# A fixed order table, two more pairs of chunks by seven block products, and six chunks converted early in an attention and two-MLP kernel

## The chip, the core and the metric

The kernel runs on one core of one Trainium2 chip. The metric is the device time of one execution in microseconds, lower is better. Before the change it is 782.16 us, the median of three runs (780.87 to 784.16).

## The reference

Memory attention with 32 slots is followed by a leaky MLP and a bilinear MLP, all in float32. `k_m` and `v_m` are per head 32 rows of 64; the second half is three large products over 2304 tokens.

```python
a = softmax(phi, axis=seq)                       # 4 x 8 x 576 x 32
k_m, v_m = a^T @ k, a^T @ v                      # per head 32 x 64
x = softmax(q @ k_m^T / 8) @ v_m                 # -> 2304 x 512
h = x @ w_in;  x = max(0.01 * h, h) @ w_out      # 512 -> 2048 -> 512
out = ((x @ w_a) * (x @ w_b)) @ w_out2           # 512 -> 1536 -> 512
```

## The kernel before

A product of two float32 matrices is done as three passes: each operand is split into a rounded high part and the rest, and high x high, high x low and low x high are summed in PSUM (`PASSES`). A split costs one copy (ACT or DVE) and one subtraction (DVE). Weights come from DRAM as 64-bit numbers and are turned into float32 by two ACT and four DVE instructions for each 128x512 piece (`weight`: high, low, clamp, shift, join, add), then split.

There are three stages. The first is attention (0 to about 60 us), batch by batch. `kv_part` loads phi, k and v, takes the maximum over the sequence (`nmx`, DVE), the exponential (ACT), transposes (`ta`, `tz`, PE), multiplies (`km`), scales (`kvn`), transposes again (`kvt`) and copies the result into `kd` and `vm`; `sc_both` makes the scores, whose softmax (`sm`, with the helpers `mx` and `sr`) ends in the tile `at`. The tokens of a batch come in two pieces, of 320 and 256 columns. The second stage is the first MLP (to about 375 us): `vw` folds `v_m` into `w_in`, `h_unit` makes a block of h, `y_unit` multiplies it by `w_out`. The third is the second MLP over 12 chunks of 128 of its 1536 columns and over two halves `s` of the tokens; the columns of 64 tokens of each batch that are left over go through `left_unit`. `ab_unit` makes both inner products of a chunk with seven block products, `abx`, `aby` and `abz`, instead of eight.

The last product, with `w_out2`, takes two chunks at a time. Where `by_seven(s, c)` is false, `o_unit` does it directly: 8 outputs of 6 passes of 512 columns. Where it is true, `p_sums` and `w2_sums` build sums of blocks of both factors, and `o_part` multiplies them with seven products for each of two row halves (3 passes each) and spreads them over the accumulators:

```python
SEVENS = ((8, 9, 10, 11), tuple(range(10)))      # chunks by seven, for s = 0 and s = 1
O_PARTS = ((1, "A11", "B11"), (2, "A12", "B21"), (6, "S2", "T2"), (7, "S3", "T3"), (4, "A22", "T4"), (5, "S1", "T1"), (3, "S4", "B22"))
```

`p_sums` forms T1 to T4 with four subtractions and splits seven operands; `w2_sums` loads the float32 weights again (`wf`), makes four sums and splits them.

The first `PRE` chunks of the second MLP have their weights converted during the first MLP, written to DRAM (`keep_weights`) and read back (`w_back`); the others are converted in the third stage.

The order of all of it is not the order of the code. Each operation is recorded with the tiles that it reads and writes (`Program.op`); `Program.order` plays the program through with assumed costs (`c_dve`, `c_act`, `c_pass`, `SLACK`, `NUDGE`), picks at each moment the most urgent operation that is ready and has room, also its engine where two can do it and the room of its tiles, and `run` issues the operations in that order. All transfers are issued by SP in program order, each one waits until the transfer eight places before it has landed. `WARM` transposes of an identity matrix stand at the head of PE's work, and `idle` puts four more behind some early results. An engine works its list strictly in that order.

Of the kernel before, what the change touches and what calls it, by code (L numbers as in the profile page):

```python
# [52 lines left out]
PRE = 5  # L53
# [4 lines left out]
NUDGE = {1: -48.49, 2: -17.57, 3: -0.76, 4: -3.51, 6: -10.66, 9: -0.3, 10: 0.34, 11: 0.67, 12: -0.23, 15: -4.91, 16: 0.37, 19: -0.01, 22: -12.61, 23: -25.92, 24: 6.05, 25: -20.43, 26: 6.22, 29: 5.25, 30: -1.03, 33: -1.08, 34: 0.18, 35: -1.25, 36: 7.2, 38: -0.74, 40: -2.21, 42: -1.91, 44: -0.72, 45: 1.51, 46: 20.7, 47: 4.08, 48: -8.63, 49: 4.68, 50: -23.08, 51: -1.24, 52: 0.28, 54: -12.45, 55: -3.05, 57: -0.08, 58: 4.38, 60: 25.62, 61: -0.19, 62: 1.46, 63: -0.19, 64: 14.35, 65: 17.46, 66: 7.11, 67: -30.82, 68: -2.57, 69: -3.68, 70: 4.08, 71: 2.16, 72: -5.51, 73: 3.76, 74: 11.57, 76: -0.33, 77: 0.8, 81: 2.6, 83: -0.23, 86: 0.21, 88: 16.61, 90: -1.17, 92: -0.59, 96: 4.63, 99: 0.07, 103: 0.97, 106: 14.54, 107: -27.63, 109: 1.17, 110: -2.34, 111: -0.09, 112: -2.83, 113: -0.93, 114: -1.13, 118: -3.12, 119: -12.84, 121: -0.12, 122: -0.26, 124: 1.93, 128: -13.55, 133: -2.46, 135: -0.09, 138: 0.06, 139: -3.54, 145: 1.03, 147: 0.04, 150: -0.64, 154: 2.61, 156: -36.26, 158: 16.1, 159: 1.35, 161: 3.36, 162: -0.42, 164: 4.55, 165: 0.05, 166: -3.77, 168: 0.39, 170: 11.14, 171: -3.97, 172: -5.44, 173: -2.43, 174: 1.13, 176: 0.94, 177: 5.17, 179: -1.18, 180: 0.4, 191: -1.73, 193: 2.21, 194: -0.27, 202: 0.73, 206: 0.97, 210: 0.09, 211: -0.24, 213: 15.62, 218: 2.9, 222: 0.72, 223: -0.03, 224: 1.55, 225: 0.27, 226: 8.51, 227: -0.23, 228: 1.22, 229: -0.49, 230: 9.69, 231: -43.15, 234: 0.36, 236: -1.75, 237: 2.72, 238: -58.33, 239: -1.64, 244: 4.13, 245: 10.87, 246: -44.04, 247: 2.64, 248: -4.48, 250: -0.39, 252: -1.44, 253: -1.5, 254: 0.23, 258: -1.35, 260: 3.26, 265: 9.59, 270: 5.29, 273: -4.26, 275: -9.82, 276: 1.34, 278: -7.31, 280: -6.24, 284: -1.88, 285: 0.18, 290: 1.13, 291: 1.14, 292: -5.63, 294: 1.39, 298: -0.06, 301: -5.57, 302: 0.42, 305: -1.09, 309: -17.67, 310: -0.78, 318: 0.61, 322: -1.59, 323: -0.28, 326: 12.04, 330: -13.23, 331: 1.15, 332: 8.66, 334: 3.29, 335: 7.89, 336: -0.53, 337: -6.49, 338: -2.42, 340: -16.79, 342: 3.52, 343: -0.05, 344: -8.26, 346: -18.18, 347: -0.13, 348: 0.63, 349: -0.21, 351: -2.03, 352: -0.87, 353: -3.55, 354: -0.99, 355: 5.28, 358: -0.8, 360: -2.83, 361: -4.43, 362: -0.31, 364: -0.25, 365: 0.37, 366: -0.51, 368: -0.28, 370: 8.22, 372: 2.75, 376: 6.22, 377: 0.07, 378: -9.41, 382: 9.32, 383: -14.31, 384: 0.6, 388: -0.21, 390: -2.09, 394: 9.89, 396: 0.61, 397: -7.48, 398: 0.4, 400: -16.99, 402: -0.43, 404: -0.91, 406: 6.5, 407: 1.68, 408: -4.78, 410: -0.5, 412: 0.42, 413: 9.97, 414: -2.31, 418: 10.12, 420: -0.66, 421: -0.48, 424: -1.62, 425: 19.33, 426: 3.26, 427: -14.35, 428: -25.92, 430: 8.73, 431: -0.14, 432: 5.62, 434: -0.05, 435: 5.56, 436: 3.43, 438: -0.46, 439: 3.09, 440: 0.69, 441: -1.61, 442: 5.28, 444: -3.22, 445: -1.01, 448: 2.67, 449: -0.8, 450: 4.58, 451: -4.01, 452: 2.12, 454: -4.52, 456: -0.86, 458: -0.99, 462: -1.59, 466: -2.13, 469: -5.99, 470: 0.23, 471: -4.55, 472: -1.36, 474: -6.92, 477: -0.94, 478: -5.9, 488: -1.13, 489: 0.2, 491: -4.41, 492: -0.47, 493: -0.58, 497: 0.08, 500: -7.25, 503: 1.25, 504: -0.9, 506: -0.19, 507: -0.2, 508: 2.0, 510: 1.27, 534: -19.4, 538: -0.38, 542: 14.1, 543: 0.63, 550: 0.74, 551: -0.99, 558: -0.88, 559: -9.51, 561: -0.16, 567: 0.56, 572: -0.2, 1281: 0.97, 1301: 0.22}  # L58
# [8 lines left out]
POOL_BIAS = 19.06
LAT, LAT_SAME, LAT_DMA = 0.427, 0.372, 6.72
OVER = {'DMA': 0.0, 'PE': 0.0, 'ACT': 0.1, 'DVE': 0.058, 'POOL': 0.0}
BLOCKED = 7.16  # L70
# [39 lines left out]
class Program:  # L112
# [13 lines left out]
    def op(self, eng, cost, fn, r=(), w=(), tiles=(), pos=None, ahead=60.0, keep=0, slack=0.0, soon=False):  # L126
        o = Op()
        port = isinstance(eng, Port)
        o.costs = {e: (c - OVER[e]) * SPARE[e] for e, c in (eng if isinstance(eng, dict) else {eng: cost}).items()}
# [23 lines left out]
    @staticmethod  # L153
    def lat(a, b):
        return LAT_DMA if a.eng == "DMA" else LAT_SAME if a.eng == b.eng else LAT

    def urgency(self, target):

        for o in reversed(self.ops):
            t = target.get(o.seq, 1e9)  # L160
            for a in o.after:
                t = min(t, a.late - self.lat(o, a) - o.cost)
            o.late = t - o.slack
        first = {}
        for o in self.ops:
            for k in o.tiles:
                if first.setdefault(k, o) is not o and self.specs[k][0] not in ("slot", "big", "five"):
                    o.late = min(o.late, max(x.late + x.cost for x in o.before) + 2.0)
            if o.soon:
                o.late = min(o.late, max(x.late + x.cost for x in o.before) + 1.0)  # L170

    def order(self, target):
        uses, free, rooms_of = {}, {}, {}
        for o in self.ops:
# [1312 lines left out]
```

## Time and profile before

| | |
|---|---|
| median of three runs | 782.16 us |
| profiled execution, device time | 781.57 us |
| its span, first to last instruction | 779.8 us |
| PE busy | 768.4 us |
| DVE busy | 632.2 us |
| ACT busy | 402.3 us |
| mean granted TensorE clock, of full speed | 0.993 |

The span is what the trace covers; the device time is 1.8 us longer than it. Instructions of one engine are pipelined, so that a busy PE is not by itself a PE at its peak; whether it is has to be read from how far apart its groups of matmuls end. A wait of an engine counts only where PE waits for it in turn.

### The profile page before, as it was taken

How to read it: one execution, taken by the hardware profiler on the slowest of the kernel's cores; microseconds unless marked ns; L12 is line 12 of the kernel's file. 1: busy time of each engine (PE TensorE's matmuls, PEld its weight loads, DVE VectorE, ACT ScalarE, POOL GpSimd, SP SyncE). 2: the span in 40 equal slices, each digit the busy share in tenths (PEclk: the TensorE clock that was granted, in tenths of full speed). 3: DMA queues.
4: the chain of work that ended last, by engine and by line, in shares of the span. 5: the costliest groups of instructions: out<-in, count | busy, mean ns of one | idle time of the engine just before them, and what ended most of it. 6: DMA issues, size and time to landing. Idle time of an engine off the chain costs nothing.

```text
span 779.8 us, 12713 instructions
## 1 busy us (share of the span) xinstructions
PE 768.4 (99%) x4762; PEld 658.2 (84%) x4762; DVE 632.2 (81%) x1205; ACT 402.3 (52%) x856; POOL 0.7 (0%) x6
## 2 busy tenths in 40 slices
PE   7899999999999999999999999999999999999998
PEld 6577898889888988898888888888888888888886
DVE  4897899789788988585742999999899777898876
ACT  4685777667457555453444546454453344444430
POOL 0000000000000000000000000000000000000000
PEclk8999999999999999999999999999999999999999
DMA  9993241755065532035975566584789886556603
GB/s 319 379 311 114 82 163 68 244 174 191 27 231 177 177 106 109 18 108 199 379 276 193 193 215 243 191 296 162 252 266 359 275 289 232 191 193 239 216 1 108
DMA packets 58860, 155.22 MB, mean 199 GB/s; under 512 B 7408, under 2 KB 22768, under 8 KB 58800
## 3 DMA queue, kind: packets, MB, share of 16 engines
q1 hardware_dynamic: 58800, 154.42, 56.2%
q8 instruction: 37, 0.61, 0.3%
q14 instruction: 23, 0.19, 0.1%
HBM read 107.74 MB, written 46.66 MB: 198 GB/s over the span
## 4 chain that ended last, share of the span: by engine, by line
PE 95%; DMA 3%; DVE 1%; SPq 0%; issue 0%
PE y L886 24%; PE abx L1107 17%; PE h L834 12%; PE o L1204 9%; PE abz L1107 8%; PE os_x L1323 5%; PE aby L1107 4%; PE os_z L1323 2%; PE b L1161 2%; PE a L1161 2%; PE y L882 2%; PE vw L765 2%; DMA phi<-in_phiT_dram 1%; PE os_y L1323 1%; DMA raw_win<-in_w_in_dram 1%; PE km L608 1%
## 5 line engine op out<-in xcount | busy, mean ns | idle before, releaser
L886 PE MATMUL y<-g,wout 128*128 128x320 f32 (+2 forms) x1104 | 199.3, 334 | 0.0
L886 PEld LDWEIGHTS y<-g,wout 128*128 128x128 f32 x1104 | 175.3, 188 | 21.1 <-issue 4.7
L1107 PE MATMUL abx<-yb_T,wo 128*128 128x512 f32 x432 | 110.2, 390 | 0.0
L1107 PEld LDWEIGHTS abx<-yb_T,wo 128*128 128x128 f32 x432 | 80.0, 188 | 15.8
L787 ACT ACTIVATE g<-h 128x320 fp32r<-128x320 f32 (+1 forms) x120 | 49.9, 416 | 68.1 <-PE h L834 63.8
L1118 ACT COPY t<-abx 128x512 f32<-128x512 f32 x72 | 42.2, 587 | 74.1 <-PE abx L1107 73.4
L834 PE MATMUL h<-ahi,vwh 128*128 128x320 f32 (+1 forms) x240 | 72.1, 300 | 0.0
L834 PE MATMUL h<-ahi,vwl 128*128 128x320 f32 (+1 forms) x240 | 71.0, 296 | 0.0
L834 PE MATMUL h<-alo,vwh 128*128 128x320 f32 (+1 forms) x240 | 71.0, 296 | 0.0
L905 DVE TENSOR_TENSOR acc<-y,acc 128x320 f32<-128x320 f32 (+1 forms) x72 | 40.1, 557 | 31.4 <-PE y L886 30.3
L850 DVE TENSOR_TENSOR g<-t,g 128x320 fp32r<-128x320 f32 (+1 forms) x120 | 53.8, 454 | 10.3 <-ACT t L787 9.4
L1204 PE MATMUL o<-p,wout 128*128 128x512 f32 (+2 forms) x246 | 59.8, 385 | 0.5 <-DVE osum L1217 0.5
L1204 PEld LDWEIGHTS o<-p,wout 128*128 128x128 f32 x246 | 45.6, 188 | 10.3 <-DVE osum L1217 1.1
L787 ACT ACTIVATE t<-h 128x320 f32<-128x320 f32 (+1 forms) x120 | 49.9, 416 | 1.5 <-PE h L834 1.2
L834 PEld LDWEIGHTS h<-ahi,vwh 128*128 128x128 f32 x240 | 45.4, 189 | 5.1 <-issue 3.0
L834 PEld LDWEIGHTS h<-alo,vwh 128*128 128x128 f32 x240 | 45.4, 189 | 0.2
L834 PEld LDWEIGHTS h<-ahi,vwl 128*128 128x128 f32 x240 | 45.5, 190 | 0.0
L1115 DVE TENSOR_TENSOR t<-abz,t 128x512 f32<-128x512 f32 x48 | 33.0, 687 | 10.5 <-PE abz L1107 5.7
L1343 ACT COPY ok<-os_x 128x512 f32<-128x512 f32 x42 | 24.6, 587 | 25.6 <-PE os_x L1323 23.3
L1107 PE MATMUL abx<-yb_B,wo 128*128 128x512 f32 x144 | 36.9, 391 | 0.0
L1107 PE MATMUL aby<-yb_B,wo 128*128 128x512 f32 x144 | 36.6, 390 | 0.0
L1107 PE MATMUL abz<-yb_B,wo 128*128 128x512 f32 x144 | 36.6, 390 | 0.0
(334 smaller groups left out, 1385.6 us busy)
## 6 DMA issues: line engine op xcount, KB each, us to landing
k_wo<-wo SPq DMA_DIRECT2D x28, 512.0 KB, 3.9
wo<-k_wo SPq DMA_DIRECT2D x28, 512.0 KB, 4.3
raw_wout<-in_w_out_dram SPq DMA_DIRECT2D x23, 512.0 KB, 5.1
raw_win<-in_w_in_dram SPq DMA_DIRECT2D x16, 512.0 KB, 6.4
kv<-in_kv_dram SPq DMA_DIRECT2D x16, 512.0 KB, 10.5
k_yb_T<-yb_T SPq DMA_DIRECT2D x8, 512.0 KB, 6.4
yb_T<-k_yb_T SPq DMA_DIRECT2D x8, 512.0 KB, 7.0
k_wout<-wout SPq DMA_DIRECT2D x7, 512.0 KB, 5.3
```

The source lines that it names most:

```text
L787: nc.scalar.activation(dst, src, AF.Prelu, alpha=0.01)
L834: nc.tensor.matmul(T[o], T[w[u]][:, k, fs], T[a[v]][:, k, cols], start=(k == 0 and i == 0), stop=(k == 1 and i == 2))
L850: lambda T, e: engines[e].tensor_tensor(T[g][:, i, 1, to], T[t], T[g][:, i, 0, to].bitcast(F32), op=ALU.subtract),
L886: nc.tensor.matmul(T[o], w[:, u, here], T[g][:, j, v, at:at + m], start=(f == 0 and p == 0), stop=(f == 3 and p == 2))
L905: "DVE", c_dve(m), lambda T: nc.vector.tensor_tensor(T[acc][:, i, :], T[o], T[acc][:, i, :], op=ALU.add),
L1107: nc.tensor.matmul(T[o], T[w][:, which, u, k * P:(k + 1) * P], T[ys[v]][:, k, :], start=first and k == 0 and x == 0, stop=k == 1 and x == ...
L1115: op("DVE", 0.69, lambda T: nc.vector.tensor_tensor(T[to], T[o], T[x], op=ALU.add), r=[o, x], w=[to], tiles=[o, x, to])
L1118: op("ACT", 0.59, lambda T: nc.scalar.copy(T[t], T[X]), r=[X], w=[t], tiles=[X, t])
L1161: nc.tensor.matmul(T[o], T[w][:, k // 2, u, k % 2 * P:(k % 2 + 1) * P], T[ys[v]][:, k, :], start=(k == 0 and x == 0), stop=(k == 3 and x = ...
L1204: nc.tensor.matmul(T[o], T[w][:, u, es], T[g][:, at, v, here], start=(x == 0 and k == 0), stop=(x == 1 and k == 2))
L1323: nc.tensor.matmul(T[o], lhs(T, u), T[g][:, v, :], start=i in (1, 2, 5) and k == 0, stop=k == 2, skip_group_check=True)
L1343: op("ACT", 0.59, lambda T: nc.scalar.copy(T[k][:, x, :], T[o]), r=[o], w=[(k, x)], tiles=[o, k])
```

## The change

The planner, its costs and `NUDGE` go. Two tables take their place: `ORDER` lists all operations by their number, with a letter for the engine where there is a choice (a ACT, v DVE, g POOL), and `PLACES` the room of each tile. `run` walks the table. Three constants change what is computed where: `SEVENS` gains chunks 0 to 3 for the first half of the tokens, two pairs; `PRE` goes from 5 to 6; `WARM` from 22 to 38 transposes.

```diff
-PRE = 5
+PRE = 6
-WARM = 22
-SEVENS = ((8, 9, 10, 11), tuple(range(10)))
+WARM = 38
+SEVENS = ((0,1,2,3,8,9,10,11), tuple(range(10)))
...
+ORDER = """
+1 238 0 26 24 246 224 25 4 5 23 6 231 239 9 2 3 27 12v 28 241v 46 247 30 31 32v 45 225 240 8 227v 34a 228 64 226 242 249v 248 44 35 243 10a 36 22 250 229 37
...
+PLACES = """
+b4 s6 s26 kvn0 g1 g0 f2 b6 b7 b5 b7 s15 s12 s19 s1 kvn0 s14 f5 b6 b7 b7 b6 s17 s4 f6 s14 kvn0 s19 s24 g5 b5 b7 b7 b5 f5 s25 kvn0 s9 f0 b6 b7 b5 b6 f3 b6 b5
...
+    def run(self, make):
+        rooms = dict(zip(self.specs, PLACES.split()))
+        engine = {"a": "ACT", "v": "DVE", "g": "POOL"}
+        tiles, done = {}, set()
+        for word in ORDER.split():
+            o = self.ops[int(word.rstrip("avg"))]
+            assert o.before <= done and o not in done
+            done.add(o)
             for k in o.tiles:
                 if k not in tiles:
-                    tiles[k] = make(k, got[k], *self.specs[k])
+                    tiles[k] = make(k, rooms[k], *self.specs[k])
             if len(o.costs) > 1:
-                o.fn(tiles, e)
+                o.fn(tiles, engine[word[-1]])
             else:
                 o.fn(tiles)
```

By count of instructions, PE loses 96 matmuls of `o` (128x512) and gains 84 of `os` and 16 transposes `warm`; DVE has 45 instructions more, ACT 9 more, SP 7 transfers more (two of `wf`, five of chunk 5's weights back from DRAM). Nearly every row of every engine stands in another place. Three places follow.

The first is SP, the loads of the opening (names end in a number of the tile; `q_0_0_0` and `q_0_1_0` are the 320 columns of batch 0, `phi_1` and `kv_1` belong to batch 1). Before, from the eighth load on:

```order
L469 DMA raw_win_0_0_131<-in_w_in_dram 128x2x256
L572 DMA kv_0_0_1_146<-in_kv_dram 128x1024
L572 DMA kv_0_0_0_155<-in_kv_dram 128x1024
L469 DMA raw_win_0_1_170<-in_w_in_dram 128x2x256
L666 DMA q_0_1_1_179<-in_qT_dram 128x2x256
L666 DMA q_0_0_1_190<-in_qT_dram 128x2x256
L666 DMA q_0_1_0_200<-in_qT_dram 128x2x320
L666 DMA q_0_0_0_212<-in_qT_dram 128x2x320
L562 DMA phi_1_225<-in_phiT_dram 128x1152
```

After, from the same place on:

```order
L530 DMA kvr_0_146<-in_kv_rest_dram 64x2x512
L621 DMA q_0_0_1_149<-in_qT_dram 128x2x256
L424 DMA raw_win_0_1_152<-in_w_in_dram 128x2x256
L527 DMA kv_0_0_0_158<-in_kv_dram 128x1024
L527 DMA kv_0_0_1_160<-in_kv_dram 128x1024
L517 DMA phi_1_167<-in_phiT_dram 128x1152
L621 DMA q_0_1_1_180<-in_qT_dram 128x2x256
L527 DMA kv_1_1_0_193<-in_kv_dram 128x1024
L621 DMA q_0_1_0_199<-in_qT_dram 128x2x320
L621 DMA q_0_0_0_216<-in_qT_dram 128x2x320
```

`phi_1` moves from the 16th to the 13th load, `q_0_0_0` from the 15th to the 17th, and `kv_0_0` from the 9th and 10th to the 11th and 12th.

The second place is DVE, behind the tile `at_0_1` with which the first MLP starts. Before:

```order
L726 STREAM_TRANSPOSE at_0_1_430<-sm_0_1_313 128x512
L717 TENSOR_REDUCE sr_0_10_84<-sm_0_0_345 128x20
L718 TENSOR_SCALAR sr_0_10_84<-sr_0_10_84 128x20
L719 RECIPROCAL sr_0_10_84<-sr_0_10_84 128x20
L626 TENSOR_SCALAR kvn_1_1_448<-km_1_1_406,er_1_82 128x256
L722 TENSOR_TENSOR sm_0_0_345<-sm_0_0_345,sr_0_10_84 128x640
L482 TENSOR_SCALAR cv_wout_0_0_434<-cv_wout_0_0_434 128x512
L726 STREAM_TRANSPOSE at_0_0_467<-sm_0_0_345 128x640
```

After, from `sm_0_0` on:

```order
L677 TENSOR_TENSOR sm_0_0_363<-sm_0_0_363,sr_0_10_84 128x640
L681 STREAM_TRANSPOSE at_0_0_465<-sm_0_0_363 128x640
L437 TENSOR_SCALAR cv_wout_0_0_460<-cv_wout_0_0_460 128x512
L491 TENSOR_REDUCE nmx_0_77<-phi_2_340 128x2
L437 TENSOR_SCALAR cv_wout_0_1_483<-cv_wout_0_1_483 128x512
L441 TENSOR_SCALAR cv_wout_0_0_460<-cv_wout_0_0_460 128x512
L441 TENSOR_SCALAR cv_wout_0_1_483<-cv_wout_0_1_483 128x512
L491 TENSOR_REDUCE nmx_1_80<-phi_3_344 128x2
L445 SCALAR_TENSOR_TENSOR cv_wout_0_1_483<-raw_wout_0_1_324,cv_wout_0_1_483 128x512
L445 SCALAR_TENSOR_TENSOR cv_wout_0_0_460<-raw_wout_0_0_293,cv_wout_0_0_460 128x512
L368 COPY kd1_75<-kvt_1_0_508 64x64 x2
```

The `kvn` of batch 1 leave DVE (ACT makes them now), both maxima `nmx` come early, and the copies of `kd1`, which were ACT's, stand behind them.

The third place is PE in the third stage, at the first pair of chunks (`abx_0_2` is chunk 2 of the first half, `o_0_0_0_0` the first direct output of chunks 0 and 1). Before:

```order
L1107 MATMUL abx_0_2_4787<-yb_0_B11_0_0_3841,wo_0_2_0_4484 128x512 x2
L1107 MATMUL abx_0_2_4787<-yb_0_B11_1_0_3849,wo_0_2_0_4484 128x512
L1107 MATMUL abx_0_2_4787<-yb_0_B11_0_0_3841,wo_0_2_0_4484 128x512
L1204 MATMUL o_0_0_0_0_4798<-p_0_0_0_4672,wout2_0_0_4505 128x512 x3
L1204 MATMUL o_0_0_0_0_4798<-p_0_1_0_4779,wout2_1_0_4520 128x512 x3
```

After, behind the unit T3 of the same chunk 2:

```order
L1062 MATMUL abx_0_2_4802<-yb_0_T3_0_0_4363,wo_0_2_3_4699 128x512 x2
L1062 MATMUL abx_0_2_4802<-yb_0_T3_1_0_4383,wo_0_2_3_4699 128x512
L1062 MATMUL abx_0_2_4802<-yb_0_T3_0_0_4363,wo_0_2_3_4699 128x512
L1278 MATMUL os_0_0_0_z_4949<-pb_0_0_T1_4814,w2_0_0_0_4779 128x512 x3
L1278 MATMUL os_0_0_0_x_4852<-pb_0_0_T3_4909,w2_0_0_1_4781 128x512 x3
```

In place of units of six matmuls of `o` stand units of three of `os`, spread between those of later chunks.

## Rows read from the trace of the kernel before

**Rows 1.** The page's head, engines and last chain.
```profile
span 779.8 us, 12713 instructions
PE 768.4 (99%) x4762; PEld 658.2 (84%) x4762; DVE 632.2 (81%) x1205; ACT 402.3 (52%) x856; POOL 0.7 (0%) x6
PE 95%; DMA 3%; DVE 1%; SPq 0%; issue 0%
```

**Rows 2.** Windows: length, PE, PEld, DVE, ACT, POOL busy, clock, DMA, GB/s.
```profile
300.00:350.00 50.00, 50.00 (x352) 44.92 (x351) 37.59 (x70) 25.33 (x59) 0.00 (x0) 1.00 0.21 76
350.00:450.00 100.00, 100.00 (x530) 87.11 (x529) 61.00 (x107) 44.32 (x86) 0.00 (x0) 1.00 0.68 249
450.00:600.00 150.00, 150.00 (x797) 129.66 (x796) 139.89 (x269) 71.39 (x131) 0.00 (x0) 1.00 0.70 244
```

**Rows 3.** One window for lines L1107, L1323, L1204 alone: PE and PEld.
```profile
600.00:700.00 100.00, 69.50 (x282) 52.36 (x281) 1.00 0.70 240
600.00:700.00 100.00, 38.84 (x147) 27.39 (x147) 1.00 0.70 240
600.00:700.00 100.00, 3.49 (x24) 3.40 (x24) 1.00 0.70 240
```

**Rows 4.** The last chain in order of time: start, length, what.
```profile
33.01 2.59 PE h L816 x12
37.76 0.70 PE sc L682 x16
38.46 2.35 PE h L816 x8
52.29 2.35 PE y L882 x8
375.88 1.36 PE abz L1107 x6
379.96 1.43 PE a L1161 x12
```

**Rows 5.** Timeline of SP's issues in the opening: start, length, what.
```profile
13.57 0.35 SPq L562 DMA_DIRECT2D phi<-in_phiT_dram  x1
21.11 1.26 SPq L469 DMA_DIRECT2D raw_wout<-in_w_out_dram  x2
24.28 2.08 SPq L660 DMA_DIRECT2D q<-in_qT_dram  x2
33.39 0.33 SPq L660 DMA_DIRECT2D q<-in_qT_dram  x1
```

**Rows 6.** Timeline of DVE in the opening.
```profile
24.28 1.35 DVE L536 TENSOR_REDUCE nmx<-phi 128x2 f32<-128x1152 f32 x1 [1.08 <-DMA phi<-in_phiT_dram]
27.15 0.51 DVE L703 STREAM_TRANSPOSE sm<-sc 128x320 f32<-128x320 f32 x1
31.35 0.48 DVE L626 TENSOR_SCALAR kvn<-km,er 128x256 f32<-128x256 f32 x1 [0.36 <-PE km L608]
31.75 0.70 DVE L726 STREAM_TRANSPOSE at<-sm 128x512 f32<-128x512 f32 x1
34.62 0.42 DVE L482 TENSOR_SCALAR cv_wout<-cv_wout 128x512 f32<-128x512 f32 x1
34.96 0.84 DVE L726 STREAM_TRANSPOSE at<-sm 128x640 f32<-128x640 f32 x1
```

**Rows 7.** Window of the first loads, columns as in Rows 2.
```profile
10.00:20.00 10.00, 8.26 (x93) 5.79 (x93) 6.08 (x15) 5.19 (x13) 0.00 (x0) 0.66 1.05 389
```

**Rows 8.** Timeline of PE at the start.
```profile
1.35 4.95 PE L430 MATMUL warm<-ident 128*128 128x128 f32 x22 [1.35 <-POOL ident masks.py:199]
12.24 1.08 PE L608 MATMUL km<-kv,en 128*32 128x128 f32 x16 [0.41 <-DMA kv<-in_kv_dram]
```

**Rows 9.** DVE groups by form: count, busy, mean ns, idle before.
```profile
L1115 DVE TENSOR_TENSOR t<-abz,t 128x512 f32<-128x512 f32 x48 | 33.0, 687 | 10.5 <-PE abz L1107 5.7 <-ACT t L1118 4.5
L1250 DVE TENSOR_TENSOR w2s<-wf 128x256 f32<-128x256 f32 x14 | 5.6, 419 | 2.6 <-PE abx L1107 2.6
```

More of the change, by code (lines that the diff above doesn't have):

```diff
@@ L1 @@
-from bisect import insort
 from contextlib import ExitStack
-from heapq import heappop, heappush
 import concourse.bass as bass
@@ L66 @@
 BIAS = 0.52
[L67 to L70, printed above, removed]
 DMA_RATE = 355000.0
-SPARE = {'DMA': 1.03, 'PE': 1.0, 'ACT': 1.03, 'DVE': 1.03, 'POOL': 0.92}
 def c_dve(n):
@@ L99 @@
+f5 b4 b3 b4 g1 s28 s25 s24 s26 s14 s28 g5 s6 s20 b7 b2 b5 t2 t4 t0 s4 b4 b3 s14 b4 g2 f6 s6 s8 f3 s6 f5 s10 g5 s22 s15 s13 s19 s15 b6 b2 b5 t1 t3 t2 s19 b4
+b3 b4 s24 s26 s14 g2 s8 s5 s2 f7 s22 g1 b1 b0 b7 t0 t4 t1 f6 s22 b4 b3 s2 b4 g0 g6 s25 s13 s28 s1 s4 b6 b0 b1 t2 t3 t1 s1 f4 b4 b3 b4 b4 b3 b4 b3 b4 b3 b4
+b3 b4 b3
+"""
 class Port(dict):
-    pass
-class NoRoom(RuntimeError):
     pass
@@ L128, in op @@
         port = isinstance(eng, Port)
-        o.costs = {e: (c - OVER[e]) * SPARE[e] for e, c in (eng if isinstance(eng, dict) else {eng: cost}).items()}
+        o.costs = eng if isinstance(eng, dict) else {eng: cost}
         eng = next(iter(o.costs))
@@ L151, in op @@
         return o
[L153 to L170, printed above, removed]
@@ L300, in run @@
-    def run(self, make, rounds=6):
-        main = [o for o in self.ops if o.pos is not None]
-        main.sort(key=lambda o: o.pos)
-        target, t = {}, START
-        for o in main:
-            target[o.seq] = t
-            t += o.cost
-        best, self.tries = None, []
-        for _ in range(rounds):
-            self.urgency(target)
-            try:
-                done, got = self.order(target)
-            except NoRoom:
-                if best is None:
-                    raise
-                break
-            end = max(o.end for o in done)
-            self.tries.append(round(end, 1))
-            if best is None or end < best[0]:
-                best = (end, done, got, [o.eng for o in done])
-                self.best_ops = [(o.start, o.end, o.seq, o.eng, o.tiles) for o in done]
-                self.best_got = got
-            target = {o.seq: o.start for o in main}
-            t = 1e9
-            for o in reversed(main):
-                t = target[o.seq] = min(target[o.seq], t - 1e-3)
-        self.length, done, got, engines = best
-        tiles = {}
-        for o, e in zip(done, engines):
+    def run(self, make):
[6 more added lines that the diff above has]
+            done.add(o)
```

257 lines of the change are left out of this document (129 added, 128 removed).

## The prediction

> **What bounds the kernel now.** I read the page's head first [rows 1]: PE is busy for 768.4 of 779.8 us and carries 95% of the chain that ended last; DVE, with 632.2 us, is next. The reader is to see that only PE's own time, and what PE waits for, can move the end. The clock is no question outside the opening: it is 1.00 in the later windows [rows 2].
>
> A busy PE need not be a PE at its peak, so the next view is the chain in order of time [rows 4]. In the third stage six matmuls of 512 columns take 1.36 us, 0.227 us each, and twelve of 256 columns 1.43, 0.119 each. Counted over 100 us [rows 3], 282 + 147 of the first and 24 of the second kind make 429 x 0.227 + 24 x 0.119 = 100.2 us: no time is left over. PE is at its peak there though DVE is busy for 139.9 of 150 us in one stretch [rows 2]. So from about 33 us to the end each matmul less is worth its whole time, and nothing else can be gained but the opening.
>
> The opening is bound otherwise. SP issues each load when the one eight places before it has landed, so its issues tell landings [rows 5]: the 8th landed at 13.57, `phi_1`, the 16th, at 24.28, the 23rd at 33.39. By the shapes, 3392 KB lie up to the 8th and 9984 KB up to the 23rd, so the loads come at 6592 / 19.82 = 333 KB/us, back to back. DVE waits 1.08 us for `phi_1` [rows 6], and the first unit of the first MLP starts at 33.01 [rows 4], behind the tile `at_0_1`, which DVE ends at 32.45 [rows 6].
>
> **Seven products for two more pairs.** PE loses 96 matmuls of `o` and gains 84 of `os`, all of 512 columns: 12 x 0.227 = 2.72 us less, on the path.
>
> DVE pays for it with some 30 wide instructions more of 0.687 us (subtractions, splits, evictions), 8 sums of 0.419 [rows 9] and a few copies, about 26 us. They fall into the first 100 us of the third stage, where DVE is idle for 39 of 100 us [rows 2]; ACT, idle for 56, takes casts. So I cost them at nothing. If that cover were gone, each `os` unit that comes late by one DVE instruction would cost PE 0.69 us, and four such units would eat the gain.
>
> [...]
>
> **Six chunks early.** Chunk 5's weights need about 11.8 us of DVE (three times clamp, shift, join and add: 6.6; four sums: 1.7; five subtractions: 3.4). They leave the stretch 450 to 600, where DVE is 93% busy, and go before 375, where the last 50 us of the first MLP alone leave 12.4 idle [rows 2]. Five loads of 512 KB more, and two of `wf`, are 3.6 MB, 9.2 us at the 389 GB/s of [rows 7], against a third of 250 us free on the queues [rows 2]. Nothing.
>
> **Sixteen more transposes at the start.** 22 took 4.95 us [rows 8], so 38 end near 9.9 instead of 6.3. Behind them stand transposes of `phi_0`; the products that need those wait for `kv` until 12.24 [rows 8]. Nothing.
>
> **The opening in its new order.** `phi_1` has 896 KB less ahead of it and lands 2.7 us earlier, at 21.6; `q_0_0_0` (landed at about 21.9, since the second issue of the pair at 21.11 waits for it [rows 5]) has 1088 KB more ahead and lands at 25.2. Its scores take 0.70 [rows 4], the two transposes behind them together about 0.93 (0.51 each, overlapping by a tenth [rows 6]), so DVE has `sm_0_0` at about 26.9, against 27.66 before (27.15 + 0.51 [rows 6]). From there to the start of `at_0_1` is 4.1 us before; the `kvn` between them, with its wait 0.76 (31.75 less the 30.99 at which that wait begins [rows 6]), is ACT's now. That ends `at_0_1` near 31.0, 1.4 us earlier. PE also needs the last `kv` of batch 1, the 21st load in both orders: 1024 KB before the 23rd, 30.3, and about one more microsecond for `km`. I put the first unit at 31.4. The like of it before is 33.01 less the `kvt` that is behind it now, 32.6: 1.2 us gained.
>
> Then some is given back. `at_0_0` ends at 35.80 before [rows 6], and with two foreign instructions less between them at about 33.6 after. The copies of `kd1` stand behind two maxima of 1.35 each [rows 6], which wait for `phi_2` and `phi_3`, the 24th and 25th load: 576 KB each behind 33.39, so 35.1 and 36.8. The first maximum ends at 36.5, three instructions of 0.42 [rows 6] at 37.7, the second maximum at 39.1, two joins of 0.69 at 40.4, the copies at 40.9. PE reaches the scores that need `kd1` after four units of 256 columns (0.86 each, from 2.59 for three), three of 320 (1.08), and 1.3 for small transposes: 31.4 + 8.0 = 39.4, and 0.4 for the exponentials of `phi_2`. It waits about 1.1 there, 1.5 in all. Queued behind those scores are `h` and `y` units of batch 0. Before had its own: eight records of 320 columns would take 2.16 by the 256-column rate and take 2.35 [rows 4], in four such pieces, 0.8 us. The opening is worth -1.2 + 1.5 - 0.8 = -0.5 us. Its ends: -2.0 if none of the new waits is there, +3 if the first unit starts 1 us later than before and the waits double.
>
> **The sum.** -2.72 - 0.5 = -3.2 us. The profiled execution took 781.57 us, 0.59 below the median of the runs; 778.35 on its scale is 778.9 on that of the median, -0.4%.
>
> **Rivals.** First, a better opening: none of the waits behind `at_0_0`, since the loads run ahead of 333 KB/us when small pieces of `q` no longer stand together. Then -2.72 - 2.0: 777.4. For it speaks that `phi_1` frees DVE early; against it that `q_0_0_0` and `phi_3` are landings, which an order on DVE doesn't move.
>
> Second, the matmuls go but their time stays: `os` units come in runs of three, and each change between two accumulators or a late `pb` makes PE wait 0.2 us or so, 56 units at 0.05 being enough. Then only the opening counts: 781.7. [...] Against it, `os` units stand in the window of [rows 3] at the full rate.
>
> Third, slower: DVE in the first 28 us. The maximum of `phi_0_1`, the fourth load now (1600 KB, so near 8.2), stands second on DVE, and all conversions of `w_in` behind it, about 11 us of work from 9.0 on. Back to back they end near 20, before `phi_1`. But DVE was busy for only 6.08 of 10 us in that stretch [rows 7]; at that share they end at 27.2, and `kvn`, `kd0`, the scores and `at_0_1` come 7 us later: 782.16 - 2.72 + 7.1 = 786.5. It decides from 6.6 us in the opening. Against it: by 9 us most of what DVE waited for has landed.
>
> **How the numbers follow.** A change of 0.5%, 3.9 us, is about what a measurement of this kernel can tell from none: faster is below 778.25, slower above 786.07. The forecast, 778.3 to 780.8 of its own, has 0.45; the better opening 0.32; the time that stays 0.15; the slow DVE 0.08. Faster is the second case and a little of the first: 0.33; slower 0.08; the rest 0.59. The range reaches from 776.2, a microsecond below the better opening, to 783.0, above the third case; the slow DVE is left out.
>
> **What would show it.** 84 more `os` and 96 fewer `o` matmuls with the spacing of 1.36 us per six unchanged. The first `h` unit near 31.4 and the copies of `kd1` near 41, with the scores waiting on them. DVE in the first 100 us of the third stage near 87% and PE still without a gap. It is wrong if PE shows waits on `pb` tiles or ACT there, if the first `h` unit starts after 33, or if the count above leaves more than 1 us of a 100 us window over.

## The result and the profile after

The kernel after takes 786.28 us (784.79 to 790.43) against 781.79 (the median of seven executions; the 782.16 at the head is that of three): ratio 1.0063, interval 1.0040 to 1.0086. A second measurement (e8 below) gave 784.55 us, ratio 1.0044 [1.0027, 1.0061]. It is slower by 3.4 to 4.9 us, where 3.2 less was forecast. The profiled execution took 787.23 us.

The page's head of the kernel after, which answers to [rows 1]:

```profile
span 785.5 us, 12755 instructions
PE 769.0 (98%) x4766; PEld 656.6 (84%) x4766; DVE 650.9 (83%) x1250; ACT 404.1 (51%) x865; POOL 0.7 (0%) x6
PE 86%; DMA 8%; DVE 3%; ACT 1%; issue 1%; SPq 0%; ACTq 0%; DVEq 0%
```

PE's share of the last chain fell from 95% to 86%, that of transfers rose from 3% to 8%. By the heads PE is idle for 16.5 us (785.5 less 769.0), where it was 11.4 before: 5.1 of the 5.7 us by which the span grew. The place to look is where PE waits. The product lines in one late window (PE and PEld as in [rows 3]; L1062 is L1107 before, L1278 is L1323, and all line numbers are 45 smaller):

```profile
660.00:760.00 100.00, 69.82 (x283) 52.80 (x282) 1.00 0.56 205
660.00:760.00 100.00, 42.17 (x159) 29.75 (x159) 1.00 0.56 205
```

283 + 159 = 442 matmuls of 512 columns x 0.227 = 100.3 us: where PE works it is at its peak as before, so the 12 matmuls that went are worth their 2.72 us. About 7 us were lost elsewhere. The opening first, PE and then DVE (the last bracket is the idle time before and what ended it). The first block is the kernel before, for comparison:

```profile
32.85 2.75 PE L816 MATMUL h<-at,vwf 128*128 128x256 f32 x12
```

```profile
8.39 0.27 PE L547 MATMUL tz<-ident,phi 128*64 128x128 f32 x1
10.79 0.66 PE L544 MATMUL ta<-ident,phi 128*128 128x128 f32 x4 [2.12 <-ACT phi L497]
...
16.20 0.65 PE L563 MATMUL km<-kvr,en 64*32 64x128 f32 x8 [3.32 <-DMA kvr<-in_kv_rest_dram]
...
27.83 1.32 PE L637 MATMUL sc<-q,kd 64*32 64x320 f32 x16 [1.05 <-DVE sm L668]
...
35.13 1.13 PE L771 MATMUL h<-at,vwf 128*128 128x256 f32 x4
```
```profile
9.08 0.75 DVE L491 TENSOR_REDUCE nmx<-phi 128x1 f32<-128x576 f32 x1 [4.68 <-DMA phi<-in_phiT_dram]
...
24.37 1.34 DVE L491 TENSOR_REDUCE nmx<-phi 128x2 f32<-128x1152 f32 x1
...
33.52 0.71 DVE L681 STREAM_TRANSPOSE at<-sm 128x512 f32<-128x512 f32 x1
...
43.07 0.46 DVE L368 COPY kd<-kvt 64x64 f32<-64x64 f32 x2 [0.77 <-ACT vm L366]
```

On the timeline the first `h` unit starts at 35.13 instead of 32.85 (33.01 in [rows 4] is its place on the chain), `at_0_1` ends at 34.2 instead of 32.45, and the copies of `kd1` end near 43.5. PE has two long waits before 17 us. The maximum of `phi_1` starts at 24.37, where it started at 24.28 before [rows 6], though `phi_1` landed 2.3 us earlier: DVE works through the conversions of `w_in` until then.

Later PE waits where it did not before. Two places, from the timelines of PE, ACT and DVE:

```profile
344.06 0.41 PE L789 MATMUL h<-ahi,vwh 128*128 128x320 f32 x1 [0.21 <-ACT t L742]
...
654.15 0.98 PE L1278 MATMUL os_x<-pb_B,wout 128*128 128x512 f32 x3 [1.67 <-ACT osum L366]
```
```profile
342.40 1.05 ACT L366 CAST yb_T<-yt_T 128x1024 fp32r<-128x1024 f32 x1 [1.60 <-DVE yt_T L896]
...
652.74 0.62 ACT L366 CAST pb_B<-pf 128x512 fp32r<-128x512 f32 x1 [5.08 <-DMA out_dram<-oacc]
```
```profile
344.74 1.23 DVE L926 TENSOR_TENSOR yb_T<-yt_T,yb_T 128x1024 fp32r<-128x1024 f32 x1 [2.03 <-DMA k_wout_-1_4190<-wout_-1_4122]
```

At 652 us the wait begins at a tile whose room a transfer still holds: `pb_B` waits for the store of a finished output, `osum` is queued behind it on ACT, and PE needs the bank that `osum` empties. At 344 us it is another: `t` is queued on ACT behind the cast of `yb_T`, which waited 1.60 us for a sum on DVE. DVE's own wait for a transfer there (the store of early converted weights) ends at 344.74, after PE had gone on.

### The profile page after: what moved, and what is told of

The parts are those of the page before. It is cut to its first block, busy times and chain, and to the rows that moved or that the text cites. A ratio compares the mean times of both kernels' runs of the same rounds, so it can differ in the third digit from the quotient of the medians.

```text
span 785.5 us, 12755 instructions
## 1 busy us (share of the span) xinstructions
PE 769.0 (98%) x4766; PEld 656.6 (84%) x4766; DVE 650.9 (83%) x1250; ACT 404.1 (51%) x865; POOL 0.7 (0%) x6
## 4 chain that ended last, share of the span: by engine, by line
PE 86%; DMA 8%; DVE 3%; ACT 1%; issue 1%; SPq 0%; ACTq 0%; DVEq 0%
PE y L841 22%; PE abx L1062 15%; PE h L789 12%; PE abz L1062 7%; PE os_x L1278 6%; PE o L1159 6%; PE aby L1062 4%; DMA kv<-in_kv_dram 4%; PE os_z L1278 3%; PE y L837 2%; PE vw L720 2%; PE b L1116 2%; PE a L1116 2%; PE os_y L1278 2%; DMA q<-in_qT_dram 1%; DMA wout<-k_wout_-1_2918 1%
## 5 line engine op out<-in xcount | busy, mean ns | idle before, releaser
L1062 PE MATMUL abx<-yb_T,wo 128*128 128x512 f32 x432 | 110.1, 390 | 0.3 <-ACT t L1073 0.2
L1062 PEld LDWEIGHTS abx<-yb_T,wo 128*128 128x128 f32 x432 | 80.2, 188 | 17.0 <-ACT t L1073 0.7
L789 PE MATMUL h<-ahi,vwh 128*128 128x256 f32 (+1 forms) x240 | 72.9, 304 | 0.5 <-ACT g L742 0.3
L742 ACT ACTIVATE g<-h 128x256 fp32r<-128x256 f32 (+1 forms) x120 | 48.6, 417 | 46.1 <-PE h L789 40.6
L789 PE MATMUL h<-ahi,vwl 128*128 128x256 f32 (+1 forms) x240 | 71.0, 296 | 0.0
L789 PE MATMUL h<-alo,vwh 128*128 128x256 f32 (+1 forms) x240 | 71.0, 296 | 0.0
L1298 ACT COPY ok<-os_x 128x512 f32<-128x512 f32 x54 | 31.6, 588 | 40.4 <-PE os_x L1278 35.6
L366 ACT CAST pb_B<-pf 128x512 fp32r<-128x512 f32 x27 | 16.8, 623 | 42.2 <-DVE pf L1089 14.9
L1062 PE MATMUL abz<-yb_B,wo 128*128 128x512 f32 x144 | 36.7, 390 | 0.0
L1062 PE MATMUL abx<-yb_B,wo 128*128 128x512 f32 x144 | 36.7, 390 | 0.0
L1062 PE MATMUL aby<-yb_B,wo 128*128 128x512 f32 x144 | 36.7, 390 | 0.0
L1062 PE MATMUL abz<-yb_T,wo 128*128 128x512 f32 x144 | 36.7, 390 | 0.0
## 6 DMA issues: line engine op xcount, KB each, us to landing
kv<-in_kv_dram SPq DMA_DIRECT2D x16, 512.0 KB, 11.4
```

Of the source, the lines that this page charges most:

```text
L742: nc.scalar.activation(dst, src, AF.Prelu, alpha=0.01)
L789: nc.tensor.matmul(T[o], T[w[u]][:, k, fs], T[a[v]][:, k, cols], start=(k == 0 and i == 0), stop=(k == 1 and i == 2))
L1062: nc.tensor.matmul(T[o], T[w][:, which, u, k * P:(k + 1) * P], T[ys[v]][:, k, :], start=first and k == 0 and x == 0, stop=k == 1 and x == ...
L1298: op("ACT", 0.59, lambda T: nc.scalar.copy(T[k][:, x, :], T[o]), r=[o], w=[(k, x)], tiles=[o, k])
```

## The experiments

Eighteen runs were made (e8 is the kernel after itself). "Old opening" means that the first 650 operations of the table (to about 75 us) have the order, engines and rooms of the kernel before; what follows is the kernel after. Ratios are to the kernel before on the same chip; 0.001 is 0.78 us.

| run | kernel | median, us | ratio [95%] |
|---|---|---|---|
| e8 | after, again | 784.55 | 1.0044 [1.0027, 1.0061] |
| e1 | after, old opening | 781.76 | 0.9996 [0.9985, 1.0008] |
| e2 | after, six stores earlier | 787.06 | 1.0072 [1.0057, 1.0088] |
| e3 | after, 22 transposes | 783.81 | 1.0031 [1.0013, 1.0049] |
| e4 | planner of before, work of after | 798.11 | 1.0207 [1.0182, 1.0233] |
| e5 | after, `kvr` in 128 partitions | 783.42 | 1.0024 [1.0007, 1.0040] |
| e6 | e1 + `kvr` in 128 | 780.78 | 0.9983 [0.9969, 0.9996] |
| e7 | e1 + other rooms | 780.74 | 0.9991 [0.9979, 1.0003] |
| e9 | before, 38 transposes | 783.52 | 1.0021 [1.0006, 1.0035] |
| e10 | e9 + `kvr` in 128 | 781.28 | 0.9993 [0.9981, 1.0005] |
| e11 | e6 + other rooms | 780.49 | 0.9988 [0.9975, 1.0002] |
| e12 | e5 + early conversions | 783.49 | 1.0019 [1.0004, 1.0035] |
| e13 | e6 with the new loads | 783.39 | 1.0026 [1.0011, 1.0040] |
| e14 | e5 with the old loads | 784.74 | 1.0044 [1.0029, 1.0060] |
| e15 | e11, 22 transposes | 779.61 | 0.9977 [0.9967, 0.9988] |
| e16 | e1, 22 transposes | 781.64 | 1.0007 [0.9990, 1.0023] |
| e17 | before + `kvr` in 128 | 780.69 | 0.9982 [0.9970, 0.9994] |
| e18 | e16 + `kvr` in 128 | 779.05 | 0.9966 [0.9952, 0.9980] |

**Opening or later stages.** Edit of e1 (the first words of the table):

```diff
-1 238 0 26 24 246 224 25 4 5 23 6 231 239 9 2 3 27 12v ...
+0 24 246 4 238 1 26 25 27 224 28 247 31 29 30 248 3 249v ...
```

Expected of e1: 

> The kernel after, with the first 650 operations (all up to about 75 us: attention, the loads, the first weights) in the order, on the engines and in the rooms of the kernel before, and 38 transposes still. If the new order of the opening is what costs 3 to 3.5 us, the first h unit starts near 33 instead of 35.1 and the time is 782.5 to 783.2. If the slow opening of the profiled run was an accident of the transfers, or if the later stages give it back, the time stays at 785.5 to 786.5.

Expected of e8: 

> The kernel after once more, unchanged, beside the others on this chip. If the 2.5 us by which e3 (22 transposes) was faster are real, it stays at 786.3; if the chip or the day made them, 783.8. In its trace the waits of PE in the third stage stand at the same places (343, 385, 497, 652 us) if they belong to the order, and at others if they hang on when the transfers land.

e1 is 3.7 us faster than e8 (1.0044 less 0.9996) and its first `h` unit starts at 31.60. So the new order of the opening costs about 3.7 us, a little more than the 3 to 3.5 expected. e8's profile has no wait at 652 us at all but keeps two short ones at 342 to 344: some waits belong to the order, others come in some executions only.

**The loads in 64 partitions.** With the old form of `kvr` the packets slow down shortly before a `kvr` lands. The GB/s line of the first 60 us, in 40 slices of 1.5 us, of the kernel after:

```profile
GB/s 0 196 384 223 304 376 422 309 170 225 382 410 409 395 371 345 161 191 298 404 391 388 427 385 421 386 167 218 274 335 401 393 404 406 380 203 247 260 357 400
```

The dips at 12 to 15, 24 to 28, 39 to 45 and 52 to 57 us (lowest slices 170, 161, 167 and 203 GB/s) stand where a `kvr` is next, with the DMA queues busy for 9 tenths throughout; the one at 4.5 to 7.5 us also stands in e5 below and is not theirs. The first two lose (230 + 175 + 239 + 209 + 102) x 1.5 us / 400 = 3.6 us against 400 GB/s; two loads of 256 KB, 0.65 us each at 400 GB/s and 1.54 at the 170 of the lower slices, would by themselves lose 2 x 0.9 (an estimate from this line), so what moves beside them is slowed as well. The edit of e5 (and of all runs from e10 on but e16, and of e6) loads the same 256 KB into 128 partitions at 2 KB; its main lines:

```diff
-tile_of(rest, "slot" if b else "five", [2, 512 if b else 640], parts=64)
+tile_of(rest, "slot" if b else "five", [2, 512 if b else 640])
-nc.sync.dma_start(T[rest][:, :, 0:512], kv_rest[b])
+nc.sync.dma_start(T[rest][:, 0, 0:512], kv_rest[b])
...
-nc.tensor.transpose(T[tz], ph(T)[:, 4 * P:S], ident)
+nc.tensor.transpose(T[tz] if g else T[tz][0:64], ph(T)[:, S - P if g else 4 * P:S], ident)
...
-n = P if t < 4 else 64
+n = slice(0, P) if t < 4 else slice(g * 64, g * 64 + 64)
...
```

Expected of e5: 

> The kernel after, with the four loads kvr (256 KB each, the last 64 tokens of k and v) going to 128 partitions at 2 KB instead of 64 partitions at 4 KB; the matmuls of km read the second half from partitions 64 to 127, and nothing else differs. In every trace so far the packets last 1.5 to 2.3 times as long for 2 to 5 us shortly before each kvr lands, and in the new order the 21st load lands at 32.3 to 32.6 us against 29.4 to 30.7 in the old. If the 64-partition form is the cause, these stretches go, the 21st load lands near 30, the first h unit comes about 2 us earlier (31.5 to 33) and the time is 783 to 784.5. If the small pieces of q are the cause, or the order of DVE and PE alone, the 21st load stays at 32.5 and the time at 786.

Expected of e6: 

> The kernel of e1 (first 650 operations as before, the rest as after) with the kvr loads in 128 partitions as in e5. If the 64-partition loads slow the transfers there as well, its first h unit comes 0.5 to 1.5 us earlier than in e1 and the time is 780 to 781; otherwise 781.8 as in e1.

The same line of e5:

```profile
GB/s 0 208 374 202 277 364 419 403 384 406 404 411 383 380 379 397 416 393 391 404 421 402 401 408 406 249 295 391 410 412 423 403 409 406 397 414 416 192 15 0
```

The dips at 12, 24 and 52 us are gone (379 to 421 GB/s from 9 to 37.5 us; a shorter one at 37.5 stays; the loads end at 56). The issue that waits for the 21st landing, SP in the kernel after and in e5:

```profile
32.59 1.70 SPq L527 DMA_DIRECT2D kv<-in_kv_dram  x2
```
```profile
28.84 1.68 SPq L525 DMA_DIRECT2D kv<-in_kv_dram  x2
```

The loads land 3.7 us earlier, as the two dips had it. The time gains less: 1.6 us in e5 against e8, 1.0 in e6 against e1, and in the later pairs 2.2 (e10 against e9), 1.4 (e17 against before) and 3.2 (e18 against e16). The form is shown as the cause of the slow packets, and as a cost in both orders. But with it gone the new order still costs 3.2 us (e5 less e6), so it is not what sets the two orders apart. Why e5's first `h` unit still starts at 34.57 is seen in the first 33 us (columns as in [rows 2]; the kernel before, after, e6, e5):

```profile
0.00:33.00 33.00, 25.20 (x289) 17.55 (x290) 20.13 (x43) 17.37 (x40) 0.70 (x6) 0.84 0.97 339
0.00:33.00 33.00, 22.89 (x246) 16.86 (x249) 18.46 (x41) 15.11 (x37) 0.70 (x6) 0.84 0.98 307
0.00:33.00 33.00, 26.72 (x315) 19.28 (x316) 21.91 (x48) 19.54 (x46) 0.70 (x6) 0.95 0.97 357
0.00:33.00 33.00, 25.89 (x260) 17.59 (x262) 18.39 (x41) 15.49 (x37) 0.70 (x6) 0.74 0.97 355
```

The granted clock is 0.74 in e5's profiled execution: by windows it is 1.00 from 9 to 12.8 us, 0.50 from 12.8 to 29.9 and 1.00 from 29.9 to 33. PE had waited there for 2.85 us until 10.93 and for 0.68 until 12.37.

That execution took 785.71 us, the median is 783.42. The time of e5's eleven executions goes with the mean granted clock of the whole execution: the five at 0.995 or more take 781.5 us on average, the five at 0.991 or less 785.1. In e12 (below) the same two groups, six and six, take 782.4 and 784.8. Among executions at 0.995 or more e5 is 1.6 us above e6 (779.9, nine executions), by the means of all of them 3.1. So about half of what the new order costs here goes with the clock. No run sets the clock, so this sorts executions and is not a test; the other half is not explained by it.

**Loads against engines.** e12 moves the transposes of `phi_0_0` and the first conversions ahead of the maximum that waits until 9 us (`8 12v 240 241v 242 243` before `27`, and `10a` before the exponential, `28`). e13 and e14 mix the two openings.

Expected of e12: 

> e5 (the kernel after with kvr in 128 partitions) with the first weights' conversions on ACT and DVE, and the transposes and copy of phi_0_0, ahead of the maximum and exponential of phi_0_1, which wait for a load until 9 us. If these engines standing behind that load, and PE idle behind them at half the clock, is the rest of what the new opening costs, the first h unit comes 1 to 2.5 us earlier than in e5 (34.6) and the time is 781 to 782.4. If the opening's end is set elsewhere, it stays at 783.4.

Expected of e13: 

> e6 (opening as before on all engines, 38 transposes, kvr in 128 partitions, rest as after) with the first 27 loads in the sequence of the kernel after (the two halves of batch 0 exchanged, since the old order begins with the other half). If the sequence of the loads is what the new opening loses, it takes 783.0 to 783.5 like e5; if the order on PE, DVE and ACT is, 780.8 like e6.

Expected of e14: 

> The other mixture: e5 (opening as after on all engines, kvr in 128 partitions) with the first 27 loads in the sequence of the kernel before, halves exchanged. If the sequence of the loads loses the time, 780.8 to 781.5; if the order on PE, DVE and ACT does, 783.0 to 783.5.

e12 took 783.49 us as e5 did. It moves the waits more than it removes them: DVE now stands for PE's first `tz`, and PE still stands for the exponential of `phi_0_1`, 3.02 us where it was 2.85 in e5:

```profile
8.21 0.28 DVE L366 COPY en<-tz 64x128 f32<-64x128 f32 x1 [4.00 <-PE tz L545]
```
```profile
11.63 0.66 PE L542 MATMUL ta<-ident,phi 128*128 128x128 f32 x4 [3.02 <-ACT phi L495]
...
31.61 1.13 PE L769 MATMUL h<-at,vwf 128*128 128x256 f32 x4
```

So it shows that the conversions behind that maximum don't decide; the wait of PE is not tested by it. In its profiled execution (781.09 us, mean granted clock 0.996 where e5's was 0.989) the `h` unit starts at 31.61.

e13 takes 3.4 us more than e6, e14 4.8 more than e6 and 1.6 more than e5 (the last within the intervals). Each half of the new opening alone costs as much as both together, 3.2, or more: the costs don't add, and the new sequence of loads loses without the new engines' order too (e13 is where its expectation for that case had it; e14 lies above both of its ranges). The clock is not the reason there, 0.9957 on average in e13 as 0.9958 in e6. What in the loads costs it stays open.

**The transposes at the start.** `WARM` alone is changed in e3, e9 and e16 (38 or 22).

Expected of e3: 

> The kernel after with 22 transposes at the start instead of 38, and nothing else. If the transposes lie beside the first loads, as the prediction costed them, nothing changes: 785.8 to 786.8. If they hold up the first transpose of phi (8.39 us instead of 6.10) and through it the whole opening, 784 to 784.8. It also shows whether the opening's slow transfers come again at the same places.

Expected of e9: 

> The kernel before with 38 transposes at the start instead of 22, nothing else. In the traces with the old order of the opening and 38 transposes (e1, e4, e7) PE runs at half the clock for 3.4 us of the first 32, with 22 (before) for 10.2, and the first h unit starts at 31.4 to 32.0 instead of 32.85. If the transposes make that difference, the time is 780.2 to 780.8; if the one trace of before was an accident, 781.5.

Expected of e16: 

> The first 650 operations and 22 transposes exactly as before, the kvr loads as before, and only what comes later as after. Against before this is the worth of two more pairs by seven products, the sixth early chunk and the later order alone. From e1 less e9 it should be a gain of about 2.0 of the forecast 2.72 us: 779.5 to 780.2. If e9's 1.7 us were chance, e16 is as e1, 781.5.

e9 turned my reading around, and e16 missed in turn: with 38 transposes the kernel before is 1.6 us slower, not faster. In its trace they end later than the first transposes of `phi` came before, which start at 7.16 instead of 6.10 us. But the products behind those still wait for `kv`, until 12.46 instead of 12.24 [rows 8], so how the delay reaches the end isn't shown:

```profile
1.35 5.97 PE L430 MATMUL warm<-ident 128*128 128x128 f32 x38 [1.35 <-POOL ident masks.py:199]
7.16 0.27 PE L592 MATMUL tz<-ident,phi 128*64 128x128 f32 x1
...
12.46 1.08 PE L608 MATMUL km<-kv,en 128*32 128x128 f32 x16 [0.91 <-DMA kv<-in_kv_dram]
```

The other pairs give 1.0 (e8, e3), 1.3 (e6, e18), 0.9 (e10, e17), 0.9 (e11, e15) and, the other way, -0.9 (e1, e16): about 0.8 us, each by itself hardly beyond its interval.

**Behind the opening.** Edit of e2: the words `2547 2554 2558 2559 2563 2564` (stores of outputs) in front of `2648` (a load). e4 is the planner with the three constants. e7 gives each tile the SBUF room of its kind that has been free longest (`PLACES` alone). e10, e11, e15, e17 and e18 combine edits shown above.

Expected of e2: 

> The kernel after, with six stores of finished outputs put ahead of three loads of 512 KB in SP's list near 632 us, and nothing else. If PE's wait of 1.67 us at 652 us is the wait for the rooms that those stores hold, it goes and the time falls by 1.6 to 1.9, to 784.4 to 784.7. If the loads behind the stores then come late for the next units, the wait only moves, and the time stays at 786.3.

Expected of e4: 

> The planner of the kernel before with the three constants of the kernel after (two more pairs by seven products, six chunks early, 38 transposes): the same operations as the kernel after in an order that the planner finds itself; its first 724 operations stand as in the kernel before. If the work is worth its 2.72 us and the table loses it, 779 to 780.5. If the work itself costs (DVE without cover in the third stage), 783 or more, with gaps of PE at the units of the first pairs.

Expected of e7: 

> The kernel of e1 with the same order on all engines, and from operation 650 on other rooms in SBUF: each tile takes the room of its kind that has been free longest, where a room whose last user is a transfer counts as free 32 operations later. In e1's trace PE loses 1.05 us at 338 us and 0.9 us at 488 to 493 us behind tiles whose room a store or load still holds. If such rooms are what eats the gain of the 12 matmuls, these go and the time is 779.5 to 780.8. If the transfers themselves are late, it stays at 781.8.

Expected of e10: 

> The kernel before with 38 transposes and the kvr loads in 128 partitions (e5's edit). It has the opening of e6 and the old work and order behind it, so e6 less this is what two more pairs by seven products, the sixth early chunk and the table's order of the later stages are worth together. If the 12 matmuls go at their full 2.72 us and 0.4 to 1.2 us of new waits stand against them, it is 782.3 to 783.1 (1.5 to 2.3 above e6's 780.78). If the new waits eat all of it in most executions, it is 779.3 to 780.8.

Expected of e11: 

> e6 (old opening, kvr in 128 partitions) with the rooms of e7. If the two edits each give their microsecond independently, 779.7 to 780.1, below both kernels; if e7's gain was chance, 780.8 as e6.

Expected of e15: 

> e11 (old opening, kvr in 128 partitions, rooms chosen anew) with 22 transposes. If the 16 transposes cost 1 to 1.7 us in the old order of the opening, as e9 says, 778.8 to 779.6, below both kernels by more than their scatter; if they cost nothing here, 780.5.

Expected of e17: 

> The kernel before with one edit, the kvr loads in 128 partitions. From e10 less e9 the edit is worth 2.2 us, from e6 less e1 1.0: 779.5 to 780.7. If the later stages of the change are worth their 2.72 us, e15 and e18, which have the same opening and this edit, are 2 us or more below it; if new waits give all of it back, they are within 1 us of it.

Expected of e18: 

> e15 with the rooms of the table left as they are (old opening, 22 transposes, kvr in 128 partitions, the rest as after). If the rooms chosen anew are worth something, it is 0.5 to 1 us above e15, 780.1 to 780.6; if not, 779.6. Against e17 it is the worth of the change behind the opening, as e16 against before.

Four pairs have the same opening and differ in what follows: e16 less before +0.5, e1 less e9 -2.0, e6 less e10 -0.8, e18 less e17 -1.3 us. Their mean, -0.9, is a third of the 2.72; the table's order and rooms of the later stages and the sixth early chunk are in it too. Where PE is never idle the gain is nearly whole. From 33 to 700 us that is so in the kernel before and in e6's profiled execution (777.42 us, the fastest of all):

```profile
33.00:700.00 667.00, 667.00 (x4137) 577.90 (x4136) 550.99 (x1065) 358.85 (x773) 0.00 (x0) 1.00 0.56 199
33.00:700.00 667.00, 667.00 (x4134) 577.34 (x4134) 567.94 (x1106) 360.90 (x778) 0.00 (x0) 1.00 0.57 204
```

From the first `h` unit to the end they take 746.9 and 744.7 us, 2.2 less. In e16's it is 746.5: PE stands there for 0.05 to 0.18 us at 379, 401, 492, 633 and 647 us, each time until ACT or DVE is done, and the matmuls beside these waits stand further apart. Other executions have a long wait for a transfer. Where one was moved, another came: in e2 the load behind the stores is late instead:

```profile
639.49 1.63 PE L1060 MATMUL aby<-yb_B,wo 128*128 128x512 f32 x6 [2.18 <-DMA wo<-k_wo_-1_4_0_3782]
```

The long waits don't come in every execution. e18's executions lie between 778.05 and 779.47 but for two, 780.73 and 783.59, and the last was the profiled one. Its PE, its ACT and its windows around 645 us:

```profile
644.95 0.84 PE L1276 MATMUL os_z<-pb_T,w 128*128 128x512 f32 x3
648.60 0.98 PE L1276 MATMUL os_x<-pb_B,wout 128*128 128x512 f32 x3 [2.82 <-ACT osum L364]
649.42 2.50 PE L1060 MATMUL abx<-yb_T,wo 128*128 128x512 f32 x6
```
```profile
647.20 0.62 ACT L364 CAST pb_B<-pf 128x512 fp32r<-128x512 f32 x1 [6.23 <-DMA out_dram<-oacc]
```
```profile
635.00:645.00 10.00, 10.00 (x46) 8.29 (x45) 6.02 (x11) 1.77 (x3) 0.00 (x0) 1.00 0.75 242
645.00:655.00 10.00, 7.18 (x25) 5.41 (x24) 5.06 (x9) 5.45 (x11) 0.00 (x0) 0.83 0.23 54
```

It is the wait of the kernel after at 652 us, 2.82 us long, and behind it the granted clock is lower too (0.83 from 645 to 655 us, 1.00 in the ten before): six matmuls of `abx` stand 2.30 us ahead of the next group (649.42 to 651.72) instead of the 1.36 of [rows 4]. e4 shows the other end: the planner puts the same work into an order with waits of 1.4 to 2.1 us at 378, 486, 488, 538 and 648 us, and takes 16 us more than e1. Those at 378, 538 and 648 stand behind transfers, the two at 486 and 488 behind DVE, which works there without a gap: in that order DVE's time is not covered. The expectation that the table loses what the planner keeps was wrong; the table is far the better order of this work. The old order is not free of them either: e9, e10 and e17 have one of 1.36, 1.57 and 1.08 us near 640, behind the store of an output. Other rooms took 0.4 us off e1 (e7) and added 0.4 to e6 (e11), both inside the intervals: the choice of rooms is not shown to matter.

e18 (old opening, 22 transposes, `kvr` in 128 partitions, the later stages of the change) beats both kernels: 779.05 us, 0.9966 [0.9952, 0.9980]. e17 shows that half of that is the load's form alone.

## Why the prediction was wrong

The forecast was 778.9 us, within 776.2 to 783.0.

- **What bounds the kernel** held: the peak spacing of PE is unchanged (1.36 us per six matmuls, as from 641.43 to 642.79 in the kernel after), and where no new wait stands the matmuls that went take 2.2 of their 2.72 us with them (e6 against the kernel before).
- **The opening in its new order** is the step that failed: "The opening is worth -1.2 + 1.5 - 0.8 = -0.5 us", with an upper end of +3. It cost 3.7 (e8 less e1), 3.2 (e5 less e6), 1.9 with 22 transposes (e3 less e16). The first error was the rate. I gave every load 333 KB/us, whatever stands next to it; `phi_1` landed at 21.92 (forecast 21.6), but `q_0_0_0` at 27.69 (25.2) and the last `kv` of batch 1 at 32.57 (30.3), behind the slow packets before the second `kvr`. The mean hid this. From there the chain ran as laid out: the scores of `q_0_0_0` start at 27.83 and take 1.32 (forecast 0.70; the granted clock is 0.50 from 28 to 31), and the two transposes behind them end at 30.15 (26.9). This explains most of the late unit in the kernel after, but not the 3.2 us that stay when the loads are mended.
- The second error was to move DVE's and PE's steps with fixed durations. In e5 the loads land before the forecast's times (`q_0_0_0` at 24.3, the last `kv` at 28.8) and the first `h` unit still starts at 34.57, with a granted clock of 0.50 until 29.9; in e12's profiled execution, with a higher mean clock (0.996 against 0.989), it starts at 31.61, where the forecast had 31.4. And `phi_1`, early as forecast, gained nothing, since DVE was still converting `w_in` until 24.4. Over all executions the mean granted clock is 0.9925 with the new engines' order (61 executions) and 0.9951 with the old (131), 4.2 us more at half speed, the 0.50 of e5's stretch. Within the kernel before, executions at 0.993 take 782.1 and at 0.996 781.3 us on average, by which this is worth some 0.7 us; by e5's two groups (3.6 us from 0.990 to 0.996) it is some 1.6. What else the new order loses stays open.
- **Sixteen more transposes**, costed at nothing, cost about 0.8 us over six pairs. They end at 7.3 us in e9 and 8.6 in the kernel after, not near 9.9. The reason given for nothing, that the products behind them wait for `kv` until 12.24 [rows 8], held in e9 (12.46); the way to the 0.8 isn't shown.
- **Seven products for two more pairs** and **six chunks early**: the matmuls went, 2.72 us. DVE grew by 18.7 us (650.9 less 632.2), where 26 were forecast, and was busy for 79 of the 100 us from 375 (forecast near 87); the longest wait of PE in that stretch is 0.23 us, for ACT. But about 1.8 us come back in the mean of the four pairs. The traces show long waits for rooms that transfers hold, in some executions, and short ones for ACT and DVE; how the 1.8 divides between them isn't measured. The free third of the DMA queues, on which "Nothing" rested, is a mean, and SP's list is strictly in order: behind the stores of e2 a load came late, and PE waited 2.18 us for it.
- **Weight loads**: PEld is at 84% before and after, and the time moved by 0.6% for reasons that this share doesn't show.
- **The sum** missed by some 7 us (6.6 by e8, 8.1 by the first measurement): the opening by 4.2 (3.7 against -0.5), the transposes by 0.8, the time given back behind the opening by 1.8.
- **The rivals**: the third gave 786.5 and the time was 786.28, but that is luck. Of its mechanism (DVE behind the maximum of `phi_0_1`) the wait is there, 4.68 us, and the conversions of `w_in` end on DVE at 24.4, between the 20 of back to back and the rival's 27.2. Yet `at_0_1` came 1.8 us later than before and not 7, and the conversions put ahead of that wait in e12 gave nothing. The second, some 0.2 us at each change between two accumulators, did not come: in the profiled execution of the kernel after three matmuls of `os_z` stand 0.69 us ahead of those of `os_x` (656.35 to 657.04; 3 x 0.227 is 0.68), and from 375 us to the end PE has two waits of 0.2 us or more, 0.23 and 1.67. Two of the signs of being wrong came: the first `h` unit after 33, and waits on a `pb` tile and on ACT.

## What to carry to other kernels

Price a reordered stretch by the rows around each moved transfer, not by the mean rate: around the 256 KB loads into 64 partitions the core moved 160 to 340 GB/s for 3 to 6 us here, where it moved about 400 otherwise. Where PE was at its peak for hundreds of us, less work gained only as long as no tile waited for a room that a queued transfer held (1.67 us of PE in the kernel after, 2.82 in e18) and no eviction came late (0.05 to 0.18 us each in e16), so look at SP's list before costing extra transfers at nothing. Test the opening and the steady part of a table apart by putting the old prefix before the new rest.

## What the runs showed of the hardware that was not expected

- Loads of 256 KB into 64 partitions at 4 KB (in batch 0 two of 2 KB each) bring the core's rate from about 400 down to 160 to 340 GB/s for 3 to 6 us in the kernel after; in e5 the same bytes into 128 partitions at 2 KB leave 379 to 421 GB/s from 9 to 37.5 us.
- In e18 a single wait of PE of 2.82 us stands in the middle of steady work, and the granted clock of the 10 us from 645 was 0.83, where the ten before and the ten behind have 1.00: the 18 matmuls of 512 columns from 649.42 to 655.13 take 5.71 us where 18 x 0.227 is 4.09, 1.6 us beside the wait itself. In the kernel after, with the wait of 1.67 us, the window from 650 to 660 has 1.00.
- 38 transposes at the start left the kernel slower than 22 in five of six pairs, though the mean granted clock of the profiled executions was mostly no lower: 0.997 against 0.996 (e1 and e16; 0.95 against 0.90 in the first 33 us), 0.997 against 0.993 (e6 and e18), 0.997 against 0.995 (e11 and e15), 0.993 against 0.991 (after and e3), 0.993 and 0.993 (e9 and before; 0.84 and 0.84 in the first 33 us), 0.991 against 0.995 (e10 and e17).
- The same kernel's executions differ by their granted clock: in e5 those at 0.991 or less take 3.6 us more than those at 0.995 or more.
